# Attention in plain float32 for two heads at once on halves of the PE array

## The chip, the core and the metric

The kernel runs on one core of a Trainium2 chip, as a single launch. The metric is the device time of one execution in microseconds (us). The engines are called as in the profile: PE is the matmul engine and PEld its weight loads, DVE the vector engine, ACT the scalar engine, POOL the third elementwise engine, SP the one that issues the DMAs. The program holds its tiles in on-chip memory of 128 partitions, and PE writes its results to eight accumulator banks (PSUM) of 512 float32 per partition.

## The reference

Eight batches of eight heads, head dimension 64, with 512 local tokens and 32 global tokens. A local query sees the 32 global keys and the local keys at most 32 positions away. A global query sees all 544 keys. The heads of a token then form a row of 512 numbers, and all 8 x 544 = 4,352 rows go through a gated feed-forward network (the FFN).

```
k_all = concatenate([k_g, k_l]); v_all = concatenate([v_g, v_l])
out_g = softmax(scale * q_g @ k_all.T) @ v_all
s_ll  = where(|i - j| <= 32, scale * q_l @ k_l.T, -1e9)
out_l = softmax(concatenate([scale * q_l @ k_g.T, s_ll])) @ v_all
x     = concatenate([out_g, out_l]), heads side by side: rows of 512
gate  = 1 / (1 + exp(-(x @ w_gate)))          # w_gate, w_val: 512 x 1536
out   = (gate * (x @ w_val)) @ w_out          # w_out: 1536 x 512
```

Inputs and output are float32. The weights reach the device as 64-bit words that it turns into float32 itself.

## The kernel before

**Precision on PE.** A matmul of plain float32 operands appears in the trace as two passes over the same moving columns, each with its own weight load. An operand in the rounded type fp32r takes one. The kernel therefore writes a number as hi + lo, two fp32r parts, and makes a product of three fp32r matmuls (hi hi, lo hi, hi lo). The FFN is made that way throughout: `xt` holds the transposed activations and `wg`, `wv`, `wo` the weights, each with a hi and a lo half.

**Chunks.** The local tokens are cut into nine chunks: chunk 0 and chunk 1 are the first and second 256 tokens of batch 0, and chunks 2 to 8 are batches 1 to 7 of 512 tokens. The 256 global rows of all batches form a last FFN chunk. The FFN of a chunk runs over 12 slices `f` of the 1,536 hidden columns. For each slice there are 12 matmuls into `bank_g`, 12 into `bank_v` (L721) and, one slice later, 3 per block of 128 tokens into `bank_o` (L735). For 512 tokens this makes 36 matmuls of 512 columns for a slice, 432 for a chunk. Between them stand the gate (ACT: tanh, exp, abs), the value (DVE: two operations), `hh` hi (ACT) and `hh` lo (POOL).

**Attention** of a chunk is done while PE runs the FFN of the chunk before it. A `local_unit` is one head and two blocks of 128 queries: scores of each block against a window of 192 or 224 keys (L345), masked maximum (`reduce`, L392), exp (L405), sums and their inverse (L356, L357), normalising, transposing the probabilities, and the product with v (`pv`). A `global_unit` is one head: 32 global queries against all keys (`sa`, L546, and `gg`, L339), softmax on 32 partitions, transposing, and the product with v (`gp`, L493).

There are two forms. Chunks 0 and 1 and the first four heads of chunk 2 are *native*: float32 operands, q and k on 64 partitions (the even head of a pair on the lower half, the odd one on the upper half), and probabilities turned by PE (L424, L425, then a copy from PSUM). The other 52 heads are *split*: ACT and POOL cut q and k (L287 to L293) and v (L319, L321) into hi and lo, so that 128 partitions hold q hi and q lo. The probabilities are transposed in 32 x 32 blocks by DVE (`tb`), written to DRAM (`pd`) and read back in the turned order (`pt`), then cut into hi and lo as well (L467, L469). `pv` uses v hi and v lo side by side as 128 weight columns and moves p hi and p lo, 256 columns. Its two halves of partitions and columns are added by ACT, DVE and POOL (L480 to L484). For 52 heads `gp` of one head is interleaved with `sa` of the next. At the end of a pair of heads `x_split` cuts the transposed attention output into the hi and lo of `xt` (L600, L602).

**Weights.** 36 blocks of weight words (12 slices of `w_gate`, `w_val`, `w_out`) are loaded and turned into hi and lo in `convert`: two operations of DVE (L235, L236), one of ACT (L238), one of DVE (L240), one of ACT (L249), one of POOL (L251). Three word buffers and two output buffers are shared by all blocks. The FFN of chunk 0 uses a slice as soon as it is there; chunk 1 and the rest find all of them.

**What sets the order.** The class `Order` simulates five engines with a written cost per step, takes the step that can start first, and emits it. Steps may ask for named resources (`att`: four PSUM banks, `s`: three score buffers, `pt`, `tb` and so on). The FFN advances a count called progress, one for each four matmuls of 512 columns, 108 for a chunk of 512 tokens and 54 for each of chunks 0 and 1. Attention steps are released at given progress: before the change chunk 2 from 19 on, one unit each 3; a later chunk from 7 before the start of the chunk ahead of it, one unit each 4. Each engine executes its emitted instructions in that order.

## Time and profile before

| | us |
|---|---|
| median of 3 runs | 1157.84 (1156.86 to 1164.7) |
| the profiled execution | 1152.93 |
| its span, first to last instruction | 1151.2 |
| PE busy | 1114.6 (97%) |
| ACT, DVE, POOL busy | 774.6, 727.0, 708.0 |

The mean granted clock of the execution is 0.992. A row of the timeline gives the start, the time from the first start to the last end, engine, line, operation, output and inputs, the size (weights as rows * columns, then the moving partitions x columns) and how many instructions are merged in it. Ends of matmuls overlap the next start, so the pitch of PE is read from start to start. A row of the windows gives a stretch, its length, the busy time of PE, PEld, DVE, ACT and POOL with the number of instructions, the granted clock, the share of the DMA engines and GB/s. A row of the groups gives line, engine, operation, names, shapes and count, then busy time, the mean duration of one in ns, and the idle time before them.

### The profile page before, as it was taken

How to read it: one execution, taken by the hardware profiler on the slowest of the kernel's cores; microseconds unless marked ns; L12 is line 12 of the kernel's file. 1: busy time of each engine (PE TensorE's matmuls, PEld its weight loads, DVE VectorE, ACT ScalarE, POOL GpSimd, SP SyncE). 2: the span in 40 equal slices, each digit the busy share in tenths (PEclk: the TensorE clock that was granted, in tenths of full speed). 3: DMA queues.
4: the chain of work that ended last, by engine and by line, in shares of the span. 5: the costliest groups of instructions: out<-in, count | busy, mean ns of one | idle time of the engine just before them, and what ended most of it. 6: DMA issues, size and time to landing. Idle time of an engine off the chain costs nothing.

```text
span 1151.2 us, 20677 instructions
## 1 busy us (share of the span) xinstructions
PE 1114.6 (97%) x6190; PEld 924.7 (80%) x6190; DVE 727.0 (63%) x2627; ACT 774.6 (67%) x1835; POOL 708.0 (62%) x735
## 2 busy tenths in 40 slices
PE   7899999999999999999999999999999999999998
PEld 5687778878887887887788787888788878888897
DVE  5778967767774777577766777577757777211122
ACT  6778977767875777677766777677776776422232
POOL 2445456777876777777867778778776787311111
PEclk9799999999999999999999999999999999999999
DMA  6667838767665765576656765586567664221143
GB/s 234 225 214 230 259 113 241 213 178 201 181 171 144 218 179 156 163 224 180 167 167 184 195 176 155 165 225 182 165 174 209 171 190 142 83 70 67 56 165 110
DMA packets 177200, 199.83 MB, mean 174 GB/s; under 512 B 108992, under 2 KB 136640, under 8 KB 177088
## 3 DMA queue, kind: packets, MB, share of 16 engines
q1 hardware_dynamic: 177088, 198.51, 58.7%
q8 instruction: 49, 0.80, 0.3%
q14 instruction: 63, 0.52, 0.1%
HBM read 159.38 MB, written 39.06 MB: 172 GB/s over the span
## 4 chain that ended last, share of the span: by engine, by line
PE 74%; issue 6%; POOL 6%; ACT 5%; DMA 5%; DVE 3%; SPq 1%; POOLq 0%; DVEq 0%; ACTq 0%
PE bank_g L721 20%; PE bank_v L721 20%; PE bank_o L735 19%; PE bank_x L345 4%; PE bank_x L546 3%; DMA qk_raw<-in_qk_dram 2%; PE bank_x L476 2%; PE bank_x L477 2%; POOL hh L676 2%; PE bank_x L493 1%; POOL pt L469 1%; POOL kl L290 1%; PE bank_x L441 1%; DMA xt<-in_w_val_dram 1%; POOL qk_hi L293 1%
## 5 line engine op out<-in xcount | busy, mean ns | idle before, releaser
L721 PE MATMUL bank_v<-xt,wv 128*128 128x512 f32 (+1 forms) x1440 | 321.9, 364 | 7.1 <-ACT ex L660 5.9
L721 PE MATMUL bank_g<-xt,wg 128*128 128x512 f32 (+1 forms) x1440 | 321.8, 366 | 4.2 <-ACT xt L600 3.5
L735 PE MATMUL bank_o<-wo,hh 128*128 128x512 f32 x1224 | 316.0, 395 | 0.8 <-POOL hh L676 0.5
L721 PEld LDWEIGHTS bank_g<-xt,wg 128*128 128x128 f32 x1440 | 242.3, 190 | 51.4 <-ACT xt L600 4.4
L721 PEld LDWEIGHTS bank_v<-xt,wv 128*128 128x128 f32 x1440 | 237.7, 189 | 52.1 <-ACT ex L660 8.9
L735 PEld LDWEIGHTS bank_o<-wo,hh 128*128 128x128 f32 x1224 | 221.0, 188 | 45.3 <-POOL hh L676 1.9
L676 POOL TENSOR_TENSOR hh<-th,hh 128x512 fp32r<-128x512 f32 (+1 forms) x120 | 135.2, 1126 | 197.7 <-ACT hh L674 193.1
L670 DVE SCALAR_TENSOR_TENSOR bank_v<-ex,bank_v 128x512 f32<-128x512 f32 (+1 forms) x120 | 72.7, 606 | 150.6 <-PE bank_v L721 143.2
L469 POOL TENSOR_TENSOR pt<-pt 128x512 fp32r<-128x512 f32 x104 | 134.5, 1294 | 28.5 <-ACT pt L467 22.0
L674 ACT CAST hh<-th 128x512 fp32r<-128x512 f32 (+1 forms) x120 | 66.4, 553 | 110.5 <-DVE th L671 101.8
L405 ACT ACTIVATE s_buf<-s_buf,nm 128x192 f32<-128x192 f32 (+1 forms) x248 | 113.9, 462 | 18.7 <-DVE nm L392 18.3
L659 ACT ACTIVATE th<-bank_g 128x512 f32<-128x512 f32 (+1 forms) x120 | 64.0, 533 | 86.1 <-PE bank_g L721 84.1
L392 DVE CUSTOM_DVE_ANT_0 s_buf<-bank_x,masks 128x192 f32<-128x192 f32 (+1 forms) x248 | 82.0, 367 | 55.9 <-PE bank_x L345 55.6
L290 POOL TENSOR_TENSOR kl<-qk_raw,qk_hi 128x736 fp32r<-128x736 f32 x52 | 92.5, 1779 | 33.9 <-ACT qk_hi L287 27.3
L484 POOL TENSOR_TENSOR x<-t 64x256 f32<-64x256 f32 x104 | 76.1, 732 | 45.4 <-DVE t L482 33.2
L482 DVE TENSOR_TENSOR t<-bank_x,t 64x512 f32<-64x512 f32 x104 | 70.3, 676 | 43.7 <-ACT t L480 43.1
L361 DVE TENSOR_SCALAR_CACHE_REDUCE s_buf<-s_buf,r 128x224 f32<-128x224 f32 (+1 forms) x223 | 87.2, 427 | 3.7
L321 POOL TENSOR_TENSOR vhl<-v_raw,vhl 128x512 fp32r<-128x512 f32 x52 | 67.1, 1290 | 32.9 <-ACT vhl L319 15.7
L480 ACT COPY t<-bank_x 64x512 f32<-64x512 f32 x104 | 60.6, 583 | 34.5 <-PE bank_x L477 19.2
L293 POOL TENSOR_TENSOR qk_hi<-qk_raw,qk_hi 64x256 fp32r<-64x256 f32 x104 | 78.4, 774 | 4.1
L671 DVE SCALAR_TENSOR_TENSOR th<-th,bank_v 128x512 f32<-128x512 f32 (+1 forms) x120 | 72.9, 607 | 11.3 <-ACT th L662 0.4
L287 ACT CAST qk_hi<-qk_raw 128x1280 fp32r<-128x1280 f32 x52 | 65.6, 1261 | 16.6 <-DMA qk_raw<-in_qk_dram 15.4
(122 smaller groups left out, 1874.6 us busy)
## 6 DMA issues: line engine op xcount, KB each, us to landing
wo<-wo_dram SPq DMA_DIRECT2D x108, 512.0 KB, 3.4
qk_raw<-in_qk_dram SPq DMA_DIRECT2D x104, 320.0 KB, 4.7
pt<-pd SPq DMA_DIRECT2D x208, 128.0 KB, 3.1
pd<-tb SPq DMA_DIRECT2D x416, 56.0 KB, 2.2
v_raw<-in_v_dram SPq DMA_DIRECT2D x52, 256.0 KB, 3.4
...
```

The lines of the kernel that those rows point to most:

```text
L290: nc.gpsimd.tensor_tensor(kl, t[:, K0:Q1], hi[:, K0:Q1].bitcast(F32), op=ALU.subtract)
L293: nc.gpsimd.tensor_tensor(hi[64:128, r], t[64:128, r], hi[64:128, r].bitcast(F32), op=ALU.subtract)
L361: nc.vector.tensor_scalar(p, p, r, None, op0=ALU.mult, op1=ALU.add, accum_out=total)
L392: nc.vector.tensor_tensor_reduce(out=s_sb[:, i, 0:w], in0=s_ps[:, i, 0:w], in1=masks[:, m:m + w], scale=-0.125, scalar=3.0e38, op0=ALU.add ...
L405: nc.scalar.activation(s_sb[:, i, 0:w], s_sb[:, i, 0:w], AF.Exp, bias=nm[:, i:i + 1], scale=-1.0, accum_out=sm[:, i:i + 1])
L469: nc.gpsimd.tensor_tensor(flat[:, 1], flat[:, 1].bitcast(F32), flat[:, 0].bitcast(F32), op=ALU.subtract)
L484: nc.gpsimd.tensor_tensor(x_part(T, x32s, col0), t0[:, :, 0], t0[:, :, 1], op=ALU.add)
L670: nc.vector.scalar_tensor_tensor(acc, ex, 1.0, acc, op0=ALU.min, op1=ALU.mult)
L671: nc.vector.scalar_tensor_tensor(th, th, 1.0, acc, op0=ALU.add, op1=ALU.mult)
L676: nc.gpsimd.tensor_tensor(hh[:, 1, 0:ntok], th, hh[:, 0, 0:ntok].bitcast(F32), op=ALU.subtract)
L721: nc.tensor.matmul(acc, w[a][:, t, fs], xt[:, c, t, x0:x0 + ntok], start=n == 0, stop=n == 11)
L735: nc.tensor.matmul(C2["o"][t], ph[:, a, t * P:(t + 1) * P], pwo[:, c], start=f2 == 0 and i == 0, stop=f2 == NF - 1 and i == 2)
```

## The change

All attention becomes native, and two heads go through PE together. The functions `keys`, `local_scores`, `x_part`, `invert`, `normalise`, `products`, `finish`, `last_products` and `x_split` disappear. `convert`, `gate`, `value`, `put_out` and `ffn_stream` stay as they were, apart from naming their PSUM bank by its slot.

- `local_unit` takes a pair of heads. The even head's q and k lie on partitions 0 to 63, the odd head's on 64 to 127; the score matmuls (now L312) alternate between the halves and write to two banks. In `pv` (now L398) all 128 partitions of probabilities are moved, the even head's product goes to PSUM partitions 0 to 63 and the odd head's to 64 to 127 of one bank, so each uses 64 of the array's columns.
- Chunks 0 and 1 turn the probabilities by PE, as before; all the others (chunk 2 too) by DVE and DRAM, but in float32 and without cutting them.
- `xt` hi and lo are made straight from PSUM (L402 on ACT or DVE, L404 on DVE). POOL keeps the `hh` lo and the weights.
- `global_unit` takes four heads, whose 32 queries each lie on four groups of 32 partitions of the same bank; softmax, five full 128 x 128 transposes and one `gp` serve all four.
- Chunk 2's attention is released from progress 40, one unit each 6; later chunks one unit each 10. Three buffers of 4 x 224 scores, one `tb`, three of qk and of v.

The core of the diff:

```diff
-EARLY = {0: (-1000, 1), 1: (-900, 1), 2: (19, 3)}
-BASE, PER = -7, 4
-HOLE = (8, 1)
+EARLY = {0: (-1000, 1), 1: (-900, 1), 2: (40, 6)}
+BASE, PER = -7, 10
...
+        yield (st := step("scores", "PE", cold + 1.0, take=["att", "att", "s"], give=qk_over(T), after=[when(("qk", ci, pr))]))
+        slots, si = st["slots"]["att"], st["slots"]["s"][0]
+        s_ps = [bank([P, 2, 256], "bank_s", i) for i in slots]
...
         for i, j in enumerate(blocks):
-            qj = ks[0][:, qcol(j) - q0:qcol(j) - q0 + P]
-            for t, (kt, k0) in enumerate(zip(ks, k0s)):
-                js = slice(k0 + KOFF[j], k0 + KOFF[j] + KWIN[j])
-                nc.tensor.matmul(s_ps[:, i, 0:KWIN[j]], qj, kt[:, js], start=t == 0, stop=t == last)
+            for e in range(2):
+                js, qj = K0 - q0 + KOFF[j], qcol(j) - q0
+                nc.tensor.matmul(s_ps[e][:, i, 0:KWIN[j]], half(t, e)[:, qj:qj + P], half(t, e)[:, js:js + KWIN[j]],
+                                 start=True, stop=True)
...
+        yield (st := step("pv", "PE", 1.1, take=["att"] + (["xt"] if new and ci != 1 else []), give=["pt"] + v_over(T),
...
+        for i, j in enumerate(blocks):
+            side = KWIN[j] - (WIN - P)
+            for w, rows in ((VM[j], P), (VS[j], side)):
+                for e in range(2):
+                    out, p = half(o_ps, e)[:, i], moving(e, i, 0 if rows == P and w == VM[j] else 1)[0:rows]
...
+                    nc.tensor.matmul(out, vt[0:rows, e, w, :], p, start=w == VM[j], stop=w == VS[j])
+        xt, xs = xts[key], slice(T["x0"] + col0, T["x0"] + col0 + 2 * P)
+        flat = o_ps.rearrange("p i c -> p (i c)")
+        yield (st := step("x hi", {"ACT": 0.33, "DVE": 0.36}))
+        (nc.scalar.copy if st["on"] == "ACT" else nc.vector.tensor_copy)(xt[:, 0, pr, xs], flat)
+        yield step("x lo", "DVE", 0.4, give=freed(slot))
+        nc.vector.tensor_tensor(xt[:, 1, pr, xs], flat, xt[:, 0, pr, xs].bitcast(F32), op=ALU.subtract)
...
+        heads = [(half(T["qk"], e), 64 * i + 32 * e) for i, T in enumerate(pair) for e in range(2)]
+        for part in range(2):
...
+            for t, p in heads:
...
+                nc.tensor.matmul(sa[p:p + 32, 2 * part:2 * part + 2], t[:, QK - SG - q0:QK - q0], view, start=True, stop=True)
...
+        for i, T in enumerate(pair):
+            vt = group["v", T["pr"]]
+            for j in range(5):
+                for e in range(2):
+                    nc.tensor.matmul(half(og, e)[:, i], vt[:, e, (VM + VS)[j], :], ptg[:, j, 64 * i + 32 * e:64 * i + 32 * e + 32],
+                                     start=j == 0, stop=j == 4)
```

How the order of instructions moves is seen at three places. In these rows stand the line, the operation, output and inputs, and the size; `x4` merges four equal ones.

PE before, in the FFN of chunk 0, where the units of two native heads happen to follow each other (L425 turns probabilities, L345 is scores, L441 is `pv`):

```order
L425 MATMUL bank_y<-ident,s_buf_107 128x128
L345 MATMUL bank_x<-qk_nat 128x192
L345 MATMUL bank_x<-qk_nat 128x224
L345 MATMUL bank_x<-qk_nat 128x192
L345 MATMUL bank_x<-qk_nat 128x224
L441 MATMUL bank_x<-pt_nat,v_nat 64x128
```

The first two rows of L345 are one head, the next two the other head, on the other half of the partitions. Elsewhere before, one head stands alone; after, each group holds two heads, one row for both heads' matmuls of a block:

```order
L312 MATMUL bank_s<-qk 128x224 x2
L312 MATMUL bank_s<-qk 128x192 x2
L398 MATMUL bank_x<-pt,v 64x128 x16
L312 MATMUL bank_s<-qk 128x224 x2
L312 MATMUL bank_s<-qk 128x192 x2
```

PE in the FFN of a later chunk, before: one head's scores and one head's `pv` between the products of `bank_v`.

```order
L721 MATMUL bank_v<-xt,wv_119 128x512 x4
L345 MATMUL bank_x<-qk_hi 128x192
L345 MATMUL bank_x<-kl,qk_hi 128x192
L345 MATMUL bank_x<-qk_hi 128x224
L345 MATMUL bank_x<-kl,qk_hi 128x224
L476 MATMUL bank_x<-pt,vhl 128x256
L477 MATMUL bank_x<-pt,vhl 128x256
L476 MATMUL bank_x<-pt,vhl 128x256
L477 MATMUL bank_x<-pt,vhl 128x256
L721 MATMUL bank_v<-xt,wv_118 128x512 x4
```

The same engine after, in the FFN of chunk 2 (L572 and L586 are the FFN's lines now, L427 `sa`, L429 `gg`, L452 and L453 transposes, L467 `gp`, all for four heads):

```order
L572 MATMUL bank_v<-xt,wv_116 128x512 x4
L427 MATMUL bank_sa<-qk 32x256 x8
L429 MATMUL bank_gg<-qk 32x32 x4
L572 MATMUL bank_v<-xt,wv_115 128x512 x4
L586 MATMUL bank_o<-wo,hh 128x512 x12
L572 MATMUL bank_g<-xt,wg_113 128x512 x4
L452 MATMUL bank_y<-ident,pg_buf 128x128 x4
L453 MATMUL bank_z<-ident,pg_buf 128x128
L572 MATMUL bank_g<-xt,wg_114 128x512 x4
L572 MATMUL bank_g<-xt,wg_113 128x512 x4
L467 MATMUL bank_og<-ptg,v 64x32 x20
L398 MATMUL bank_x<-pt,v 64x128 x8
```

Groups of scores, `sa`, `gg`, `gp` and `pv` stand between full-array matmuls of the FFN, fewer and larger than before.

DVE before, in the second half of the weight conversion (L235, L236, L240 are the conversion, L670 and L671 the FFN's value, the rest attention of chunks 1 and 2):

```order
L235 TENSOR_SCALAR bank_w<-xt 128x512
L236 SCALAR_TENSOR_TENSOR bank_w<-xt,bank_w 128x512
L561 TENSOR_SCALAR mg<-sg 32x1
L562 RECIPROCAL mg<-mg 32x1
L240 SCALAR_TENSOR_TENSOR xt<-xt,bank_w 128x512
L235 TENSOR_SCALAR bank_w<-xt 128x512
L236 SCALAR_TENSOR_TENSOR bank_w<-xt,bank_w 128x512
L444 COPY x_1184<-bank_x 64x256
L240 SCALAR_TENSOR_TENSOR xt<-xt,bank_w 128x512
L392 ISA s_buf_107,nm<-bank_x,masks 128x224
```

After, in the same part (L231, L232 and L236 are the conversion, L520 and L521 the value):

```order
L236 SCALAR_TENSOR_TENSOR xt<-xt,bank_w 128x512 x2
L520 SCALAR_TENSOR_TENSOR bank_v<-ex,bank_v 128x256
L521 SCALAR_TENSOR_TENSOR th<-th,bank_v 128x256
L231 TENSOR_SCALAR bank_w<-xt 128x512
L232 SCALAR_TENSOR_TENSOR bank_w<-xt,bank_w 128x512
L236 SCALAR_TENSOR_TENSOR xt<-xt,bank_w 128x512
L231 TENSOR_SCALAR bank_w<-xt 128x512
L232 SCALAR_TENSOR_TENSOR bank_w<-xt,bank_w 128x512
L231 TENSOR_SCALAR bank_w<-xt 128x512
L232 SCALAR_TENSOR_TENSOR bank_w<-xt,bank_w 128x512
L236 SCALAR_TENSOR_TENSOR xt<-xt,bank_w 128x512 x2
```

The attention of chunks 0 and 1 is over by then and that of chunk 2 has not begun, so only conversion and value remain.

560 lines of the change are left out of this document (196 added, 364 removed).

## The prediction

> **What bounds the kernel now.** I read the engine totals first, then the windows between the output stores, then single stretches of PE's timeline. The rows show the engine totals, five windows, and the issues of the output stores.
>
> ```profile
> PE 1114.6 (97%) x6190; PEld 924.7 (80%) x6190; DVE 727.0 (63%) x2627; ACT 774.6 (67%) x1835; POOL 708.0 (62%) x735
> ...
> 0.00:47.00 47.00, 34.97 (x188) 27.13 (x189) 31.74 (x107) 32.96 (x89) 15.35 (x31) 0.89 0.70 241
> 47.00:155.00 108.00, 106.58 (x738) 84.78 (x736) 88.24 (x276) 91.17 (x248) 48.85 (x46) 0.98 0.69 222
> 174.50:250.30 75.80, 71.28 (x505) 63.58 (x504) 52.32 (x206) 55.60 (x142) 53.80 (x58) 1.00 0.76 215
> 377.60:502.50 124.90, 122.70 (x646) 101.99 (x645) 87.35 (x331) 90.67 (x207) 93.61 (x97) 1.00 0.64 180
> ...
> 1010.00:1090.00 80.00, 80.00 (x347) 1.00 0.19 66
> ...
> 174.40 0.88 SPq L693 DMA_DIRECT2D out_dram<-ob  x2
> 250.24 0.81 SPq L693 DMA_DIRECT2D out_dram<-ob  x2
> 377.57 1.30 SPq L693 DMA_DIRECT2D out_dram<-ob  x3
> 879.64 1.42 SPq L693 DMA_DIRECT2D out_dram<-ob  x3
> 1098.79 1.44 SPq L693 DMA_DIRECT2D out_dram<-ob  x3
> ```
>
> PE is busy nearly throughout, so what changes the length of its queue changes the time. The stretch from 1010 to 1090 holds the FFN alone: 80/347 = 0.2305 us per 512-column matmul, so a chunk's 432 take 99.6 us. Chunks 3 to 6 end every (879.64 - 377.57)/4 = 125.5 us; the other 26 us are attention and waits. The last stretch, from 1001 on, holds no attention and does not change.
>
> The FFN of chunk 0 stands out: it begins at 47 and stores at 174.40, although its matmuls (12 slices of 24 half-length and 6 whole ones) need only 12 x (24 x 0.115 + 6 x 0.2305) = 50 us. It waits for weights, the last of which is finished at 155:
>
> ```profile
> L251 POOL TENSOR_TENSOR wo<-xt,wo x12: 1269/1278/1301, 28.0 to 155.0; 128x512 fp32r<-128x512 f32 x12
> ```
>
> PE was not idle in that time, because the slow native attention of chunks 0, 1 and half of 2 filled it.
>
> **What attention costs PE now, and what two at once cost.** These rows of PE's timeline are the split form (scores, `pv`, global, each with the row behind it), then the native form.
>
> ```profile
> 208.20 0.25 PE L345 MATMUL bank_x<-qk_hi 128*128 128x192 f32 x1
> ...
> 208.64 1.56 PE L735 MATMUL bank_o<-wo,hh 128*128 128x512 f32 x6
> ...
> 213.89 0.31 PE L476 MATMUL bank_x<-pt,vhl 128*128 128x256 f32 x1
> ...
> 214.40 1.09 PE L735 MATMUL bank_o<-wo,hh 128*128 128x512 f32 x4
> ...
> 217.61 0.19 PE L493 MATMUL bank_x<-ptg,vhl 128*128 128x64 f32 x1
> ...
> 218.24 0.71 PE L721 MATMUL bank_v<-xt,wv 128*128 128x256 f32 x4
> ...
> 107.99 0.97 PE L345 MATMUL bank_x<-qk_nat 64*128 64x224 f32 x4
> 108.94 0.88 PE L493 MATMUL bank_x<-ptg_nat,v_nat 128*64 128x32 f32 x10
> 109.75 0.74 PE L721 MATMUL bank_v<-xt,wv 128*128 128x256 f32 x4
> 110.42 1.05 PE L546 MATMUL bank_x<-qk_nat 64*32 64x256 f32 x4
> 111.40 1.19 PE L721 MATMUL bank_v<-xt,wv 128*128 128x256 f32 x8
> ...
> 114.50 0.27 PE L424 MATMUL bank_y<-ident,s_buf 128*128 128x128 f32 x1
> 114.61 0.27 PE L425 MATMUL bank_y<-ident,s_buf 128*128 128x128 f32 x1
> 114.82 0.98 PE L345 MATMUL bank_x<-qk_nat 64*128 64x192 f32 x8
> 115.73 0.43 PE L441 MATMUL bank_x<-pt_nat,v_nat 128*64 128x128 f32 x2
> 116.00 0.38 PE L442 MATMUL bank_x<-pt_nat,v_nat 128*64 128x128 f32 x2
> 116.21 0.38 PE L441 MATMUL bank_x<-pt_nat,v_nat 128*64 128x128 f32 x2
> ```
>
> Split, per head: scores of two blocks 0.44, `pv` 0.51, global 0.63 plus two short `gg` (0.05). A chunk has 16 units and 8 globals: 16 x 0.95 + 8 x 0.68 = 20.6 us. With the FFN that is 120.2, so 5.3 of the 125.5 us are waits; 2.2 of them show as idle PE (124.90 - 122.70).
>
> Native, two things show. First, four score passes of one head take 0.95 us (107.99 to 108.94), and eight passes of two heads on the two halves take 0.91 (114.82 to 115.73): both halves of the rows work at once. Second, a change between full and part array costs about 0.1: L425 begins 0.11 after L424, but the part-array L345 begins 0.21 after L425. The Trainium skill ("TensorE: Matmul & The Clock Gate", section "Part 3: Packing small matmuls") has matmuls start and end strictly in program order. The trace disagrees: the program has one head's four passes ahead of the other's, and the eight still fit the time of four. By that rule the odd head's half would start one pass late in each group, an estimate of 8 x (0.2 + 0.1) = 2.4 us more per chunk than the sum below.
>
> After, per chunk on PE:
> - scores, 8 groups of two heads: from the expected end of L425 (114.72) to 115.73, 1.01 with both changes of array: 8.1, against 16 x 0.44 = 7.0 before.
> - `pv`, 8 groups. One head's pass is (116.21 - 116.00)/2 = 0.105, and there are 8 for it. If the column halves run together as the row halves do, 8 x 0.105 plus 0.06 at the start (115.73 to 116.00 is 0.27, not 0.21) plus two changes is 1.10: 8.8, against 8.2 before. If they take turns, 1.94. No row of before has both column halves in use, so the bounds are these two. I take the first, by the nearest row, that of the row halves.
> - `sa`: a pass is (111.40 - 110.42 - 0.1)/4 = 0.22. Four heads have 16, on four separate quarter-width parts. All four at once: 4 x 0.22, with `gg` and changes 1.2. By row halves alone 2.15. One at a time 4.1. I take 1.2, since parts that share neither rows nor output partitions are the same case as the row halves, and keep the rest as rivals.
> - `g turn`, five full transposes: 0.54. `gp`: a short pass is (0.81 - 0.2)/10 = 0.06; 20 pairs and the changes 1.4, or 2.6 in turn.
> - Two globals of four heads: 2 x 3.1 = 6.3, against 5.4.
>
> Sum 23.2, which is 2.6 more than before: plain float32 is no cheaper for PE in a later chunk. It has to come from waits. Of 5.3 us, those on the added halves, on `pt` lo and on `xt` (POOL, and ACT's splits) have no instruction any more. POOL keeps only `hh` lo; ACT and DVE lose the splits, the additions and most of the small softmax. I take 2 us of waits left, between 0.5 and 5.3. A later chunk is then 99.6 + 23.2 + 2 = 124.8, a change of -0.7 (-2.2 to +2.6), and chunks 3 to 7 give -3.5 (-11 to +13). The write and read of `pd` and the loads on SP are further ahead than before (one unit each 10 of progress instead of each 4, two heads in it), so I cost them at nothing: the FFN's matmuls of some 10 us between two units hide them. If that cover is gone, `pv` stands at the head of PE's queue until `pt` has landed, the FFN behind it, and the 2 us grow.
>
> **The first 250 us.** The end of the conversion sets the end of chunk 0. It needs DVE most:
>
> ```profile
> L236 DVE SCALAR_TENSOR_TENSOR bank_w<-xt,bank_w 128x512 uint32<-128x512 uint32 x36 | 25.1, 696 | 1.2
> L235 DVE TENSOR_SCALAR bank_w<-xt 128x512 uint32<-128x512 uint32 x36 | 24.7, 685 | 6.9 <-DMA xt<-in_w_val_dram 3.0 <-DMA xt<-in_w_gate_dram 2.8 <-ACT x L444 0.9
> L240 DVE SCALAR_TENSOR_TENSOR xt<-xt,bank_w 128x512 uint32<-128x512 uint32 x36 | 24.0, 677 | 5.0 <-POOL wo L251 2.3 <-POOL wg L251 1.2 <-ACT xt L238 0.8
> L392 DVE CUSTOM_DVE_ANT_0 s_buf<-bank_x,masks 128x224 f32<-128x224 f32 x124 | 47.3, 382 | 14.7 <-PE bank_x L345 14.5
> L392 DVE DVE_READ_ACCUMULATOR2_ANT nm<- 128x1 f32 x256 | 21.0, 82 | 0.0
> L356 DVE TENSOR_SCALAR r<-sm 128x1 f32<-128x1 f32 x256 | 31.6, 146 | 36.6 <-ACT s_buf L405 35.0
> L670 DVE SCALAR_TENSOR_TENSOR bank_v<-ex,bank_v 128x256 f32<-128x256 f32 x36 | 15.2, 422 | 45.0 <-PE bank_v L721 40.2 <-ACT ex L660 3.8 <-ACT pg_buf L564 1.0
> ```
>
> A block costs 0.685 + 0.696 + 0.677 = 2.06 of DVE, 36 of them 74. Before, DVE is busy 31.74 + 88.24 = 120 us until 155, which is 77% of the time. After, it must do until then: 74; for 8 units of two heads four reduces (0.382 + 0.082), five small operations of 0.146 and one x lo (as L670, 0.42), 3.0 each, 24; value of chunk 0, 12 x 2 x 0.42 = 10; two globals, 3. Together 111, and some of the normalising and copying that either engine may do, say 3. The half of chunk 2's attention that lay in this time (and 6 of 8 global softmaxes) is gone from it. At 77% this ends at 114/0.77 = 148, with a full DVE at 114. In the second half only conversion and value are left in DVE's queue, 3 x 2.06 + 0.84 = 7.0 us a slice, where a slice now takes (155.0 - 28.0)/11 = 11.5. I take 141, nearer to the first, since ACT and the two output buffers stay in the chain of each block. PE has no backlog of attention then: chunk 0 stores some 4 us later instead of 19.4, at 145.
>
> Against this stands the clock. PE will idle between slices, and a short idle costs clock: here 2.81 us of work in 5 were followed by a window at 0.55 and one at 0.50 (columns: window, length, PE, PEld, DVE, ACT, POOL, clock):
>
> ```profile
> 35.00:40.00 5.00, 2.81 (x20) 2.05 (x18) 3.99 (x7) 3.15 (x6) 2.02 (x2) 1.00 0.90 311
> 40.00:45.00 5.00, 4.97 (x20) 3.22 (x20) 4.57 (x17) 3.12 (x8) 3.23 (x3) 0.55 0.79 271
> 45.00:50.00 5.00, 4.04 (x19) 3.53 (x18) 3.27 (x9) 3.71 (x9) 0.73 (x1) 0.50 0.65 213
> ```
>
> At half clock a slice of chunk 0 takes 8.4 us instead of 4.2, about what conversion takes too, so PE still keeps up, and only the last slice is late. DVE's value steps wait for PE, and the next block's words are queued behind them. I take 1.5 us: chunk 0 stores at 146.5, -28 (-20 to -34).
>
> Chunk 1 then needs 50 us of FFN and all of chunk 2's attention but the quarter that is released before (from 40 of 54, over 60): 17 to 18, and 3 of waits: 71 against 75.8, -5. Chunk 2 took 377.57 - 250.24 = 127.3; like the others now, 124.8, -2.5.
>
> **Sum.** -28 - 5 - 2.5 - 3.5 = -39 against the profiled 1152.93: 1114. The median of the runs is 4.9 us above that execution, so 1157.84 - 39 = 1119 for the runs.
>
> **The rivals.**
> 1. *Column halves take turns.* Nothing in the trace shows them together, and both halves read the same 128 partitions, unlike the row halves. `pv` grows by 8 x 0.84, `gp` by 2 x 1.2: 9.1 us a chunk. In chunks 0 and 1 PE has room for it; for the seven chunks 2 to 8 it is 64: 1183, slower. It decides once the halves overlap less than four tenths (39 of 64 lost). Chance 0.10.
> 2. *`sa` runs two at a time.* Fourteen globals x 0.95 = +13: 1132. Chance 0.12.
> 3. *`sa` runs one at a time*, because all four heads write to one bank; the score matmuls, which overlap in the trace, write to two. 14 x 2.9 = +41: 1160, no change. Chance 0.06. The Trainium skill ("TensorEngine Tiling (Array Packing)", section "Restrictions and Gotchas") says that different row tiles cannot access the same PSUM bank simultaneously, which speaks for this; no run here shows it yet.
> 4. *The conversion does not speed up:* DVE stands at value steps for a PE at half clock. Early gain 10 instead of 28: 1137. Chance 0.10.
>
> **How the numbers follow.** The forecast has 0.62 with its own range of 1104 to 1136 (the early gain by +8 or -6, the later chunks by -8 or +12 to either side). With rivals 2 and 4 it gives faster 0.84; rival 3 is 0.06 for within 1%; rival 1 is 0.10 for slower. The runs of before spread over 0.7%, so about 1% can be told from no change. The range is 1104 to 1142: it leaves out rivals 1 and 3 and a little of the edges.
>
> **What will show it.** Right: the last weight block ends near 141 and chunk 0 stores near 146; eight `pv` passes' time for sixteen (L398 about 1.1 us from start to start with its changes); `sa` with `gg` about 1.2; later chunks end each 124 to 126 us; POOL busy falls below 250. Wrong: L398 near 1.9, L427 at 2 or more, a last weight block after 150, or PE idle in the later chunks on `pt` read back late.

## The result and the profile after

The changed kernel takes 1121.22 us (median of 4 runs, 1118.58 to 1123.63); the kernel before, run beside it, 1157.35 (4 runs, 1156.65 to 1164.70). The ratio is 0.967 with a 95% interval of 0.963 to 0.972. The profiled execution after took 1118.58 with a span of 1116.6; before, 1152.93 and 1151.2. The spans are 34.6 us apart.

The engine totals on the page after:

```profile
PE 1079.9 (97%) x6838; PEld 859.7 (77%) x6838; DVE 530.1 (47%) x1864; ACT 492.1 (44%) x1297; POOL 182.8 (16%) x171
```

A window of before that the prediction did not show, from 47 to the store of chunk 0:

```profile
47.00:174.40 127.40, 125.98 (x879) 100.21 (x878) 100.26 (x329) 104.33 (x288) 57.42 (x54) 0.99 0.62 202
```

The windows after: the start, from 47 to the store of chunk 0, the second half of the conversion, chunk 1, and chunk 3:

```profile
0.00:47.00 47.00, 34.76 (x328) 27.64 (x329) 37.11 (x163) 37.15 (x110) 10.85 (x22) 0.93 0.77 260
47.00:144.30 97.30, 77.31 (x529) 65.82 (x528) 80.51 (x190) 66.75 (x157) 45.88 (x41) 0.88 0.74 246
60.00:136.00 76.00, 56.01 (x308) 47.17 (x307) 62.88 (x128) 50.49 (x111) 39.36 (x35) 0.84 0.79 266
144.30:219.40 75.10, 75.10 (x664) 64.01 (x664) 43.51 (x181) 39.14 (x126) 8.81 (x12) 1.00 0.79 251
345.10:469.90 124.80, 124.80 (x764) 96.61 (x763) 57.89 (x220) 51.39 (x137) 15.48 (x12) 1.00 0.52 161
```

After, the issues of the output stores, from the timeline, and then the group of the `wo` weight blocks on POOL, with the durations and the first and last start:

```profile
144.30 1.04 SPq L543 DMA_DIRECT2D out_dram<-ob  x2
219.43 0.87 SPq L543 DMA_DIRECT2D out_dram<-ob  x2
345.14 1.46 SPq L543 DMA_DIRECT2D out_dram<-ob  x3
469.91 1.45 SPq L543 DMA_DIRECT2D out_dram<-ob  x3
844.54 1.45 SPq L543 DMA_DIRECT2D out_dram<-ob  x3
```

```profile
L247 POOL TENSOR_TENSOR wo<-xt,wo x12: 1276/1286/1299, 23.7 to 136.2; 128x512 fp32r<-128x512 f32 x12
```

PE's busy time fell by 1114.6 - 1079.9 = 34.7 us, as much as the span. That the two agree is chance: up to the store of chunk 1 PE's busy time fell by 45 us (232.2 to 187.2) and the time by 30.8, and behind it PE's busy time rose by 10 while the time fell by 3.8. Most of the gain lies ahead of the store of chunk 0: 174.40 became 144.30, which is 30.1 of the 34.6. Chunk 1 takes 75.1 after it (before 75.8), chunk 2 125.7 (127.3), chunks 3 to 6 (844.54 - 345.14)/4 = 124.85 each (125.5). The last weight block begins at 136.2 instead of 155.0, which is 18.8 of the 30.1; the other 11.3 are the way from there to the store, 8.1 instead of 19.4. Of the 18.8, 5.1 are there when the fourth `wo` block begins (66.6 instead of 71.7); the other 13.7 come from there to the last block, which takes 69.6 us instead of 83.3.

The limit of this stage changed. Before, from 47 to the store, PE stood idle for 1.4 us of 127.4. After, it stands idle for 20 of 97.3, with the clock at 0.84 from 60 to 136, and waits for weights. These are the rows of the waits from 60 to 125, PE's and then those of the DMA queue (a load of weight words, L222, waits for the last DVE operation on its buffer):

```profile
PE bank_g L572 <- POOL wg L247: 9.5, 7, 2.0
...
PE bank_g L572 <- ACT wg L245: 6.3, 5, 2.1
```

```profile
SPq L222 <- DVE xt L236: 39.4, 18, 5.5
```

In the later chunks (345 to 845) the view of waits has no row for PE's matmuls at all. The groups of two and four heads are these, in the timeline of PE after:

```profile
347.79 1.56 PE L572 MATMUL bank_v<-xt,wv 128*128 128x512 f32 x6
349.27 1.10 PE L398 MATMUL bank_x<-pt,v 128*64 128x128 f32 x16
350.30 1.20 PE L586 MATMUL bank_o<-wo,hh 128*128 128x512 f32 x4
351.43 0.97 PE L312 MATMUL bank_s<-qk 64*128 64x192 f32 x8
352.33 0.96 PE L586 MATMUL bank_o<-wo,hh 128*128 128x512 f32 x3
...
372.62 2.14 PE L586 MATMUL bank_o<-wo,hh 128*128 128x512 f32 x8
374.69 1.07 PE L427 MATMUL bank_sa<-qk 64*32 64x256 f32 x16
375.58 0.24 PE L429 MATMUL bank_gg<-qk 64*32 64x32 f32 x8
375.75 3.06 PE L572 MATMUL bank_g<-xt,wg 128*128 128x512 f32 x12
...
383.95 1.10 PE L398 MATMUL bank_x<-pt,v 128*64 128x128 f32 x16
384.88 1.31 PE L467 MATMUL bank_og<-ptg,v 128*64 128x32 f32 x40
386.12 0.73 PE L586 MATMUL bank_o<-wo,hh 128*128 128x512 f32 x2
```

Sixteen `pv` passes of two heads take 350.30 - 349.27 = 1.03 us; sixteen `sa` passes of four heads 375.58 - 374.69 = 0.89, with `gg` 1.06; forty `gp` passes 1.24.

### The profile page after: what moved, and what is told of

It reads as the page before. It is cut to its first block, busy times and chain, and to the rows that moved or that the text cites. A ratio compares the mean times of both kernels' runs of the same rounds, so it can differ in the third digit from the quotient of the medians.

```text
span 1116.6 us, 18791 instructions
## 1 busy us (share of the span) xinstructions
PE 1079.9 (97%) x6838; PEld 859.7 (77%) x6838; DVE 530.1 (47%) x1864; ACT 492.1 (44%) x1297; POOL 182.8 (16%) x171
## 4 chain that ended last, share of the span: by engine, by line
PE 84%; issue 4%; DMA 2%; POOL 1%; DVE 1%; ACT 0%; POOLq 0%; DVEq 0%; ACTq 0%
PE bank_v L572 24%; PE bank_g L572 24%; PE bank_o L586 23%; PE bank_x L398 5%; PE bank_s L312 5%; DMA xt<-in_w_gate_dram 2%; PE bank_og L467 2%; PE bank_sa L427 1%; POOL hh L526 1%; PE bank_y L452 1%; DMA xt<-in_w_out_dram 1%; DVE xt L236 0%; POOL wo L247 0%; POOL wg L247 0%; DVE bank_w L231 0%
## 5 line engine op out<-in xcount | busy, mean ns | idle before, releaser
L572 PE MATMUL bank_g<-xt,wg 128*128 128x512 f32 (+1 forms) x1296 | 301.7, 377 | 19.5 <-POOL wg L247 11.6
L586 PE MATMUL bank_o<-wo,hh 128*128 128x512 f32 x1224 | 314.0, 398 | 0.3 <-ACT hh L524 0.2
L572 PE MATMUL bank_v<-xt,wv 128*128 128x512 f32 (+1 forms) x1296 | 301.0, 379 | 1.3 <-POOL wv L247 0.7
L572 PEld LDWEIGHTS bank_g<-xt,wg 128*128 128x128 f32 x1296 | 226.8, 191 | 73.9 <-POOL wg L247 13.3
L572 PEld LDWEIGHTS bank_v<-xt,wv 128*128 128x128 f32 x1296 | 226.7, 193 | 53.0 <-issue 8.6
L586 PEld LDWEIGHTS bank_o<-wo,hh 128*128 128x128 f32 x1224 | 224.5, 189 | 55.0 <-issue 8.3
L520 DVE SCALAR_TENSOR_TENSOR bank_v<-ex,bank_v 128x512 f32<-128x512 f32 (+1 forms) x120 | 73.8, 615 | 257.6 <-PE bank_v L572 244.1
L524 ACT CAST hh<-th 128x512 fp32r<-128x512 f32 (+1 forms) x120 | 66.8, 557 | 163.4 <-DVE th L521 163.1
L321 DVE CUSTOM_DVE_ANT_0 s_buf<-bank_s,masks 128x192 f32<-128x192 f32 (+1 forms) x256 | 81.0, 370 | 104.6 <-PE bank_s L312 104.5
L340 DVE TENSOR_SCALAR_CACHE_REDUCE s_buf<-s_buf,r 128x192 f32<-128x192 f32 (+1 forms) x215 | 80.9, 426 | 1.7
L521 DVE SCALAR_TENSOR_TENSOR th<-th,bank_v 128x512 f32<-128x512 f32 (+1 forms) x120 | 73.0, 608 | 15.6 <-ACT pg_buf L442 0.5
L398 PE MATMUL bank_x<-pt,v 128*64 128x128 f32 (+1 forms) x1024 | 71.2, 279 | 0.2 <-ACT pt L358 0.2
L398 PEld LDWEIGHTS bank_x<-pt,v 128*64 128x64 f32 (+1 forms) x1024 | 55.0, 136 | 19.4 <-issue 11.6
L512 ACT ACTIVATE th<-th 128x512 f32<-128x512 f32 (+1 forms) x120 | 68.2, 568 | 0.0
L312 PE MATMUL bank_s<-qk 64*128 64x192 f32 (+1 forms) x512 | 64.4, 366 | 0.4 <-DVE xt L404 0.4
L365 DVE STREAM_TRANSPOSE tb<-s_buf 128x896 f32<-128x896 f32 x56 | 62.2, 1110 | 3.2 <-DMA pd<-tb 0.7
L510 ACT ACTIVATE ex<-bank_g 128x512 f32<-128x512 f32 (+1 forms) x120 | 63.6, 530 | 0.0
L312 PEld LDWEIGHTS bank_s<-qk 64*128 64x128 f32 x512 | 42.9, 188 | 21.2 <-issue 13.9
L404 DVE TENSOR_TENSOR xt<-bank_x,xt 128x256 fp32r<-128x256 f32 x64 | 26.9, 422 | 67.0 <-ACT xt L402 66.9
```

The costliest lines, as they stand in the source:

```text
L312: nc.tensor.matmul(s_ps[e][:, i, 0:KWIN[j]], half(t, e)[:, qj:qj + P], half(t, e)[:, js:js + KWIN[j]], start=True, stop=True)
L321: nc.vector.tensor_tensor_reduce(out=s_sb[:, 2 * e + i, 0:w], in0=s_ps[e][:, i, 0:w], in1=masks[:, m:m + w], scale=-0.125, scalar=3.0e38, ...
L340: nc.vector.tensor_scalar(src, src, r[:, k:k + 1], None, op0=ALU.mult, op1=ALU.add, accum_out=sm[:, k:k + 1])
L398: nc.tensor.matmul(out, vt[0:rows, e, w, :], p, start=w == VM[j], stop=w == VS[j])
L512: nc.scalar.activation(th, th, AF.Abs)
L520: nc.vector.scalar_tensor_tensor(acc, ex, 1.0, acc, op0=ALU.min, op1=ALU.mult)
```

## The experiments

All in one table first: when the last `wo` block begins on POOL, the stores of chunks 0, 1 and 2 in the profiled execution, and the time. Where there is a ratio it is to the kernel before run beside it, whose median was 1157 to 1163 us in the several sets. The stores are those of one execution, and the changed kernel's four runs spread over 5 us, so differences of a few us between two rows are read from the stages and not from the time.

| kernel | last block | chunk 0 | chunk 1 | chunk 2 | time, us | ratio (95%) |
|---|---|---|---|---|---|---|
| before | 155.0 | 174.40 | 250.24 | 377.57 | 1157.35 | |
| after | 136.2 | 144.30 | 219.43 | 345.14 | 1121.22 | 0.967 (0.963 to 0.972) |
| b_late | 156.8 | 172.24 | 278.69 | 403.70 | 1172.32 | 1.012 (1.006 to 1.019) |
| b_split_late | 163.4 | 172.10 | 278.27 | 404.36 | 1188.78 | 1.027 (1.021 to 1.034) |
| a_early | 143.2 | 156.77 | 224.38 | 348.93 | 1121.94 | 0.967 (0.963 to 0.971) |
| a_double1 | 144.7 | 152.44 | 227.64 | 353.35 | 1127.44 | one run |
| a_noword | 132.1 | 138.64 | 214.36 | 340.07 | 1113.17 | one run |
| a_words4 | 131.5 | 143.56 | 219.18 | 344.88 | 1116.11 | 0.958 (0.955 to 0.961) |
| a_words4_warm | 130.0 | 142.35 | 217.68 | 343.39 | 1116.64 | 0.964 (0.957 to 0.971) |
| a_lead9 | 177.8 | 202.91 | 223.16 | 347.67 | 1121.96 | 0.967 (0.959 to 0.975) |
| a_lead6 | 175.3 | 190.09 | 220.65 | 345.15 | 1118.46 | 0.964 (0.957 to 0.970) |
| a_words4_l8 | 167.6 | 188.22 | 213.00 | 337.50 | 1112.06 | 0.961 (0.955 to 0.966) |
| a_samecols | 145.2 | 158.35 | 239.62 | 372.24 | 1180.20 | one run |
| a_headorder | 140.0 | 146.78 | 226.51 | 356.69 | 1152.58 | one run |

### Does the kernel before gain by the later release alone, or by splitting all of chunk 2?

```diff
-EARLY = {0: (-1000, 1), 1: (-900, 1), 2: (19, 3)}
+EARLY = {0: (-1000, 1), 1: (-900, 1), 2: (40, 2.5)}
```

> The kernel before with one number pair changed: chunk 2's attention released from progress 40, one step each 2.5, instead of 19 and 3, so that it lies behind most of the weight conversion, as in the changed kernel. Theory (the early gain is PE's shorter queue, since one-head native attention is gone): nothing of PE's work goes away here, and PE had only about 6 us of idle time between 47 and 250, so chunk 0 stores some 10 to 20 us earlier, chunk 1 takes as much longer, chunk 1's store stays within 4 us of 250, and the total stays within 5 us of 1157. Rival (the gain comes from the later release alone, by taking chunk 2's work out of DVE's queue during the conversion): chunk 1 stores at 225 to 235 and the total falls to 1130 to 1140.

And with the same release, `NATIVE_HEADS = 0` instead of 4:

> The kernel before with the later release (progress 40, one step each 2.5) and with the first four heads of chunk 2 in the split form like all other heads of the later chunks. Theory: PE loses 8 native local units (about 2.2 us against 0.95) and 4 native globals (about 2.4 against 0.7), together about 17 us of a queue that was full, so chunk 2 stores 8 to 17 us earlier and the total is 1140 to 1149: half or less of the gain of the changed kernel, the rest being the one-head native work of chunks 0 and 1. Rival (splits of q, k, v on ACT and POOL were what held the early stage): with four more heads to split nothing is gained or it gets slower, 1155 to 1170.

Both take longer than before, b_late by 1.2% and b_split_late by 2.7%. Both expectations of the theory missed: the first had put the total within 5 us of 1157 and chunk 1's store within 4 us of 250, the second (1140 to 1149) is off by 40 us. The rival of the first, a gain from the later release alone, missed as well. In the profiled execution moving alone gives chunk 0 only 2 us. But in b_late's profile the first `wo` block began at 38.1 instead of 28.0; the instructions of all engines are in the order of before up to there, and its other three runs were 8 to 13 us shorter than the profiled one, so that is not the edit's. Without those 10 us chunk 0 would store some 12 us earlier than before, an estimate that agrees with the theory's 10 to 20. From the fourth to the last weight block it needed 74.9 us against 83.3 before. So chunk 2's attention did slow the conversion, by about 8 us. But chunk 1 then takes 106.5 us instead of 75.8. The first row shows that stage of b_late: of the 30.7 us, 20.0 are PE's busy time (91.28 instead of 71.28, with chunk 2's attention in it and the clock at 0.89), and 10.6 are idle time. Where PE is idle stands in its waits, of b_late from 230 to 280, then of b_split_late from 60 to 280; the last row is a window over b_split_late's chunk 1, where POOL is busy for 76.58 us:

```profile
172.30:278.70 106.40, 91.28 (x605) 78.91 (x606) 62.31 (x253) 71.53 (x185) 63.06 (x68) 0.89 0.58 163
```

```profile
PE bank_x L476 <- POOL pt L469: 9.4, 2, 7.9
```

```profile
PE bank_x L476 <- POOL pt L469: 19.4, 9, 6.8
```

```profile
174.50:278.30 103.80, 79.62 (x527) 70.80 (x526) 69.00 (x279) 72.81 (x181) 76.58 (x84) 0.85 0.69 187
```

`pv` waits for the lo half of the probabilities from POOL. A later chunk of before keeps POOL busy for 93.6 us; a chunk 1 of 75 us can't hold that. This speaks for the following reading, which is argued from the waits and not shown by a run of its own: the split form can't be squeezed into the early stage; the native form, which needs no POOL, can, but fills PE. The two-head form asks nothing of POOL for attention and less of PE than native. For the second run the rival holds, by more than it had said: splitting more heads makes it slower. That PE's queue had been full is not contradicted, since these two kernels traded it for another wait.

### Is the place of chunk 2's attention what matters?

```diff
-EARLY = {0: (-1000, 1), 1: (-900, 1), 2: (40, 6)}
+EARLY = {0: (-1000, 1), 1: (-900, 1), 2: (19, 7)}
```

> The changed kernel with chunk 2's attention released from progress 19, one unit each 7, instead of 40 and 6, about where the kernel before released it. Theory (the conversion, paced by DVE, now ends chunk 0, and PE idles about 20 us beside it): some four units of two heads enter DVE's queue in the conversion, about 5 us of DVE each, so chunk 0 stores 8 to 20 us later, chunk 1 takes 6 to 9 us less (PE work of those units now lies in its idle time), and the total is 1121 to 1133. Rival (the conversion's loads set its pace and DVE has room): chunk 0's store moves by less than 4 us and the total falls by 4 to 8, to 1113 to 1117.

Chunk 0 stores 12.5 us later, chunk 1 takes 67.6 instead of 75.1, and the time is the same (1121.94 and 1121.22). This is as the theory had it. The release moves work between the two stages; it is not where the gain comes from.

### Does PE's queue still count in the first stage?

In the four loops that issue scores, `pv`, `sa` and `gp`, each matmul of chunk 1's attention stands twice:

```diff
-            for e in range(2):
+            for e in [0, 1] * (2 if ci == 1 else 1):
```

> The changed kernel with every matmul of chunk 1's attention (scores, pv, sa, gp) issued twice, with the same results: 4 x (0.9 + 1.0) + 2 x (0.9 + 1.2) = 11.8 us more of PE inside the weight conversion, nothing more on DVE, ACT or in the loads. Theory (PE idles about 20 us beside the conversion, so PE's queue no longer sets the end of chunk 0): chunk 0 stores 0 to 4 us later than 144.3 and the total is 1121 to 1126. Rival (PE's queue still sets it, and the gain is simply PE time saved in the first 250 us): chunk 0 or chunk 1 ends 10 to 12 us later and the total is 1130 to 1134.

Chunk 0 stores 8.1 us later, between the two expectations and nearer to the rival. The rows of POOL's fourth `wo` block show where, first after, then with the doubled matmuls:

```profile
66.62 1.29 POOL L247 TENSOR_TENSOR wo<-xt,wo 128x512 fp32r<-128x512 f32 x1 [3.02 <-ACT wo L245]
```

```profile
75.43 1.30 POOL L247 TENSOR_TENSOR wo<-xt,wo 128x512 fp32r<-128x512 f32 x1 [3.87 <-ACT wo L245]
```

All 8.8 us are there by the fourth block. From it to the last block it takes 69.2 us, against 69.6 in the changed kernel. The last of the doubled groups starts at 70.1. So until about 70 us, while attention of chunks 0 and 1 goes through PE, DVE and ACT, PE's time counts. Of the time after that this run says nothing, since no doubled matmul lies there; that PE waits for weights there shows in its 20 us of idle time.

### What sets the pace of the conversion after that?

One of DVE's two first operations on a block left out:

```diff
-        nc.vector.tensor_scalar(v, high, 0x80000000, None, op0=ALU.bitwise_and)
-        nc.vector.scalar_tensor_tensor(v, low, 29, v, op0=ALU.logical_shift_right, op1=ALU.bitwise_or)
+        nc.vector.tensor_scalar(v, low, 29, None, op0=ALU.logical_shift_right)
```

> The changed kernel with one of DVE's three operations for a weight block left out: the sign bit is not taken over, so all weights are positive and the output is not the reference's; the loads, the other operations and the FFN are the same. It takes 36 x 0.69 = 25 us from DVE, 17 of them after 60. Theory (DVE sets the pace of the conversion, 63 of 76 us busy from 60 to 136): the last weight block ends 10 to 17 us earlier, at 120 to 127 instead of 137, chunk 0 stores at 127 to 135, the total is 1101 to 1111. Rival (the three word buffers and their loads set the pace): the last block ends less than 5 us earlier and the total stays within 5 us of 1121.

This kernel leaves out the sign of the weights. Of DVE's work after 60, 17 us are gone, and the last block comes only 4.1 us earlier, as the rival had it; 2.1 of the 4.1 are there at the fourth block already (64.5 instead of 66.6). The profiled execution is 1118.58 - 1113.17 = 5.4 shorter; the time of 1113.17 lies between the two expectations. DVE is the busiest engine there (62.88 of 76), but its busy time does not set the pace. The next candidate was the loop of a word buffer, since the loads wait 39.4 us of 65 for a buffer:

```diff
-    conv_bufs = [words[:, i * 1024:(i + 1) * 1024] for i in range(3)]
-    conv_out = [words[:, 3072 + i * 512:3072 + (i + 1) * 512] for i in range(2)]
+NW, NO = 4, 2
...
+    conv_bufs = [words[:, i * 1024:(i + 1) * 1024] for i in range(NW)]
+    conv_out = [ffn.tile([P, 512], U32, name="xt", tag="ob", bufs=3) for i in range(NO)]
```

> The changed kernel with four word buffers for the weight conversion instead of three (the two output buffers move into the not yet used output tiles). Theory, new after the run without one DVE operation (the loop of one word buffer sets the pace: load about 5 us from issue to landing, three DVE steps and one of ACT with their queues, three buffers): loads are issued a block earlier, DVE no longer waits for them, slices from the fourth to the last take 7.3 to 8 us each instead of 8.7, the last weight block ends at 128 to 133 instead of 137.5, the total falls to 1111 to 1117. Rival (the DMA engines are the limit, 0.7 to 0.8 busy in this stretch): the last block ends at 136 or later and the total stays within 4 us of 1121.

The last block begins 4.7 us earlier; from the fourth on a slice takes (131.5 - 67.7)/8 = 7.98 us instead of (136.2 - 66.6)/8 = 8.70. That is the theory's reading, at its weak end. The time is 1116.11 and the ratio 0.958, just below the interval of the changed kernel, which was measured in another set. Yet the profiled executions show only 0.7 us of it at chunk 0's store, since the way from the last block to there grew from 8.1 to 12.1. So the number of buffers is a part of the pace. The rest is not settled; with a DMA share of 0.96 from 80 to 100 in this kernel a fifth buffer may not help, which was not tried.

Whether the clock makes that last stretch long was the next question. Ten matmuls on old weights, whose result is overwritten, stand ahead of each of the slices 3 to 11:

```diff
+                            if C["ci"] == 0 and f >= 3 and which == 0:
+                                for i in range(10):
+                                    nc.tensor.matmul(acc, wg[0][:, i % KT, 0:P], xt[:, 0, i % KT, x0:x0 + ntok], start=True, stop=True)
```

> The kernel with four word buffers, and in chunk 0's FFN ten more matmuls of 256 columns ahead of each of the slices 3 to 11: they use old weights, write to the accumulator that the slice's first matmul then overwrites, and wait for nothing of the conversion; the result is the same. About 9 x 1.15 = 10 us of PE in time that was idle. In the kernel with four word buffers the clock from 120 to 140 was 0.75 and chunk 0 stored 10.8 us after the last weight block, against 6.8 with three. Theory (the clock falls because PE idles between slices, and the last slices then run slowly): the clock between 80 and 140 is 0.95 or more, chunk 0 stores 5 to 7 us after the last weight block, at 137 to 140, total 1110 to 1114. Rival (the added matmuls lie ahead of the slices in PE's queue and delay them, or the clock falls all the same): chunk 0 stores no earlier than 143, total 1116 to 1124.

The clock from 120 to 140 was 0.83 instead of 0.75, the way from the last block to the store 12.4 instead of 12.1, and the time the same (1116.64 and 1116.11). The time is the rival's, and chunk 0's store at 142.35 lies between the two expectations (137 to 140, and 143 or later). But the run does not test what it was made for. These are PE's wait in the last slice and the stretch behind it, first of a_words4, then with the added matmuls:

```profile
130.26 3.44 PE L575 MATMUL bank_v<-xt,wv 128*128 128x256 f32 x12 [2.93 <-ACT wv L248]
```

```profile
130.00:136.00 6.00, 5.61 (x20) 4.47 (x22) 3.17 (x8) 1.57 (x4) 3.24 (x3) 0.51 0.69 213
```

```profile
128.76 0.79 PE L578 MATMUL bank_v<-xt,wv 128*128 128x256 f32 x4 [2.89 <-ACT wv L248]
```

```profile
130.00:136.00 6.00, 5.89 (x21) 4.51 (x22) 2.16 (x6) 0.41 (x1) 2.02 (x3) 0.50 0.82 251
```

The added matmuls stand ahead of `bank_g`, while the last long wait, 2.9 us, lies between `bank_g` and `bank_v`. So it stayed, and with it the six us at half clock behind it. PE works through nearly all of them, and but for 0.1 us in a_words4 and 0.6 in a_words4_warm it has no further wait until the store. At full clock the same work would take about half, so the clock costs close to 3 us there, an estimate. In a_words4 these six us lie behind the start of the last block (131.5), in the changed kernel ahead of it (136.2), where the clock is 1.00 from 137 to 143; that is the larger part of the 4 us by which the way to the store grew with the fourth buffer. Whether a filled wait would keep the clock up is not shown.

### Can PE's idle time be used?

`LEAD = 9` and `LEAD = 6` instead of 12: the FFN of chunk 1 begins inside the conversion.

> The changed kernel with the FFN of chunk 1 begun inside the weight conversion: chunk 0 runs slices 0 to 8, chunk 1 the same slices, then both in turn for slices 9 to 11, and those last three slices are converted without an accumulator bank as scratch. Theory (conversion ends chunk 0, and PE idles some 20 us beside it): PE fills part of that idle time with chunk 1's slices, chunk 1 stores at 207 to 215 instead of 219.4, total 1109 to 1117. Rival (the conversion is slowed by chunk 1's value steps on DVE and by the missing scratch banks): chunk 1 stores at 217 to 230, total 1119 to 1132.

> The same with six slices ahead instead of nine: half of chunk 1's FFN (25 us of PE) may run inside the conversion, which fills all of PE's idle time there. Theory: chunk 1 stores at 200 to 212, total 1102 to 1114, faster than with nine. Rival: six slices without scratch banks and with chunk 1's value steps between them delay the last weight block from 137 to 150 or later; chunk 1 stores no earlier than with nine.

Neither gains more than its interval: 1121.96 and 1118.46. With nine the rival held; with six chunk 1 stores 2.5 us earlier than with nine, still outside the theory. The conversion of the last slices is slow (last block at 175 to 178); whether by the missing scratch banks or by chunk 1's steps between them is not taken apart. And a new wait appears in front of chunk 2. This is PE's row in a_lead6 from 170 to 222:

```profile
PE bank_x L398 <- DMA pt<-pd: 12.3, 3, 4.9
```

It is the wait that the prediction had costed at nothing as long as the FFN covers it. Here less FFN is left to cover it. The last run joined four word buffers and three output buffers with `LEAD = 8` and a release of chunk 2 from 30:

> Four word buffers and three output buffers, eight slices of chunk 0 and then of chunk 1 before the last four in turn, and chunk 2's attention released from progress 30 instead of 40 (with six and nine slices ahead PE waited some 12 and 8 us for chunk 2's probabilities to be read back, just before chunk 2). Theory: those waits go, PE's idle time in the conversion is filled, chunk 1 stores at 205 to 213 instead of 219, total 1102 to 1110. Rival (the slices without scratch banks, 13 to 15 us each instead of 9, and the earlier chunk 2 delay the conversion): chunk 1 stores at 217 or later, total 1115 to 1125.

```profile
PE bank_x L401 <- DMA pt<-pd: 9.2, 2, 6.5
```

1112.06 us (1110.56 to 1113.82). It is the lowest time of all, between the two expectations; the wait for `pt` is still there, 9.2 us from 170 to 215. It lies below the changed kernel in every run, by 9 us of the medians, though the two were not run side by side and the intervals of their ratios overlap by a little. In the profiled executions 6.4 us of it are there at chunk 1's store.

### What are the halves of the columns worth?

Both heads' `pv` to PSUM partitions 0 to 63:

```diff
-        o_ps = bank([P, 2, P], "bank_x", slot)
+        o_ps = bank([64, 2, 2, P], "bank_x", slot)
...
-                    out, p = half(o_ps, e)[:, i], moving(e, i, 0 if rows == P and w == VM[j] else 1)[0:rows]
+                    out, p = o_ps[:, e, i], moving(e, i, 0 if rows == P and w == VM[j] else 1)[0:rows]
```

> The changed kernel with the probability products of both heads of a pair on the same half of the array's columns: both results go to PSUM partitions 0 to 63, side by side, and are then taken from there to xt by twice as many copies of half the partitions. Theory (in the changed kernel the two column halves run at the same time): the group of 16 passes takes about 1.95 us instead of 1.10, which is 8 x 0.84 = 6.7 us for a chunk and 47 for chunks 2 to 8; a later chunk takes 131 to 132 instead of 124.9, the total 1165 to 1172. Rival (the halves took turns already, or PE has room): no change beyond 5 us.

```profile
376.37 1.97 PE L398 MATMUL bank_x<-pt,v 128*64 128x128 f32 x16
378.26 1.21 PE L589 MATMUL bank_o<-wo,hh 128*128 128x512 f32 x4
...
372.24 1.43 SPq L546 DMA_DIRECT2D out_dram<-ob  x3
...
899.23 1.45 SPq L546 DMA_DIRECT2D out_dram<-ob  x3
```

A group takes 378.26 - 376.37 = 1.89 us instead of 1.03, and a chunk (899.23 - 372.24)/4 = 131.75, 6.9 more. Over the stages of chunks 1 to 7 this is (1027.73 - 158.35) - (966.32 - 144.30) = 47.4 us, as expected. Another 14.1 lie ahead of chunk 0's store, which nobody had priced. They can't be put down to PE alone: the edit also doubles the copies to `xt`, of half the partitions each, and the groups of attention stand in another order there. In this single run the time is 1180.2, above the kernel before.

### Does the order of the heads' matmuls matter?

In the four groups all matmuls of one head come ahead of the next head's:

```diff
-        for i, j in enumerate(blocks):
-            for e in range(2):
+        for e in range(2):
+            for i, j in enumerate(blocks):
```

> The changed kernel with PE's instructions of a group in another order: all matmuls of one head, then all of the next head, in scores, pv, sa and gp, instead of the heads in turn. Theory (a matmul may pass an earlier one that uses other rows, columns or quarters of the array, as the eight score passes of two heads in the trace of before, which stood one head behind the other and took the time of four): each group takes the same time to 0.2 us, a later chunk 124 to 127, total 1116 to 1135. Rival (matmuls begin strictly in program order, so only the last pass of a head overlaps the first of the next): scores 0.7, pv 0.7, sa and gp together 2 to 4 us longer each, 16 to 19 us a chunk, total 1230 or more.

```profile
421.69 1.59 PE L398 MATMUL bank_x<-pt,v 128*64 128x128 f32 x16
423.21 0.96 PE L572 MATMUL bank_g<-xt,wg 128*128 128x512 f32 x3
...
448.49 1.09 PE L427 MATMUL bank_sa<-qk 64*32 64x256 f32 x16
449.38 0.26 PE L429 MATMUL bank_gg<-qk 64*32 64x32 f32 x8
...
356.69 1.78 SPq L543 DMA_DIRECT2D out_dram<-ob  x3
...
874.18 1.42 SPq L543 DMA_DIRECT2D out_dram<-ob  x3
```

Neither expectation: a chunk takes (874.18 - 356.69)/4 = 129.4, 4.5 more. `sa` is unchanged at 0.89 and so are the scores (0.91 against 0.90, medians of chunks 3 to 6); `pv` takes 423.21 - 421.69 = 1.52 instead of 1.03, which is 8 x 0.49 = 3.9 of the 4.5. In all, this order costs 1152.58 - 1118.58 = 34 us between the two profiled executions, about as much as the whole change gained, by a single run. Where a head has four passes, the next head's start at once; where it has eight, they don't. The starts of the 16 `pv` passes, in ns from the first (from single records of the trace, the groups at 383.95 in the changed kernel and at 421.69 in this one; in the second row a pass is put to a head by its distance of about 110 to the head's pass before):

```
heads in turn:      0   7 | 160 167 | 270 276 | 379 385 | 488 495 | 597 604 | 706 713 | 820 826
one head, the next: 0 160 270 383 491 | 497 603 657 711 766 820 880 | 988 1100 1208 1316
```

The second head's first pass starts at 497, together with the first head's fifth (491), when three of the first head's passes have not started. With four passes a head, three have not started either when the next head begins. So passes of another part of the array may overtake; that they do so past three waiting ones of a part and no more fits both cases.

## Why the prediction was right, and where it was not

**The sum.** Forecast -39 against the profiled execution, measured 1152.93 - 1118.58 = -34.4; 1119 for the runs, measured 1121. That the last two are only 2 us apart is in part luck: the sum is 4.6 off (chunk 1 gave 4 us less than forecast, chunk 0 2 more), and the median of the changed kernel lies 2.6 above its profiled execution, where 4.9 had been added.

**Chunk 0, -28 (-20 to -34).** Measured -30.1. The last block was put at 141 and began at 136.2; the way to the store was put at 5.5 and took 8.1. That PE's backlog goes was right: idle 1.4 us before, 20 after. The step that failed is the reason for the conversion's pace, "it needs DVE most": with 25 us of DVE's work gone the last block came only 4.1 us earlier, with one more word buffer 4.7. So the 77% of DVE's time that the estimate rested on did not mark the limit. A part of the limit is the loop of the word buffers (8.70 us a slice with three, 7.98 with four); the rest stays open. That the number came out nearly right is luck in part: chunk 2's attention in the conversion did cost time, 8 us by b_late and 7 by a_early, but why, if DVE's busy time does not set the pace, is not shown. Less in DVE's queue may also let that loop turn faster; this is argued.

The clock was put at 1.5 us. These rows of the changed kernel show the stretch ahead of the store, and what PE does behind it:

```profile
130.00:136.00 6.00, 5.15 (x22) 5.05 (x23) 4.65 (x17) 5.30 (x17) 2.08 (x2) 0.50 0.69 253
```

```profile
138.17 1.08 PE L572 MATMUL bank_g<-xt,wg 128*128 128x256 f32 x8
139.19 1.10 PE L398 MATMUL bank_x<-pt,v 128*64 128x128 f32 x16
...
142.15 1.55 PE L586 MATMUL bank_o<-wo,hh 128*128 128x512 f32 x6
```

PE has no wait from 130.85 to the store, and 5.15 us of that are at half clock. Half of it, 2.6 us, is the most that a full clock could have saved; but the last `wv` block ends on POOL only at 133.4, and behind that 2.7 us are left at half clock, so about 1.4 us is the nearer estimate, close to the 1.5. The slow stretch ends as the last block begins, so the 8.1 us are another term that was too small: the plain 4 us of way, which had been put without parts. In PE's order the first 24 products of chunk 1 and a `pv` group stand ahead of the last six of chunk 0, and these alone take 142.15 - 138.17 = 4.0 us.

**Chunk 1, -5; measured -0.7.** The step that failed is the sum of 50 us of FFN, 17 to 18 of attention and 3 of waits. These are PE's groups of the FFN in that stretch (144.3 to 219.4), with shapes kept apart:

```profile
L586 PE MATMUL bank_o<-wo,hh 128*128 128x512 f32 x72 | 19.9, 402 | 0.0
L572 PE MATMUL bank_v<-xt,wv 128*128 128x256 f32 x132 | 18.2, 282 | 0.0
L572 PE MATMUL bank_g<-xt,wg 128*128 128x256 f32 x127 | 17.8, 284 | 0.0
...
L572 PE MATMUL bank_g<-xt,wg 128*128 128x512 f32 x15 | 3.8, 396 | 0.0
...
L572 PE MATMUL bank_v<-xt,wv 128*128 128x512 f32 x12 | 3.2, 404 | 0.0
```

By pitch this is 259 x 0.115 + 72 x 0.2305 + 27 x 0.2305 = 52.6 us, since 27 matmuls of chunk 2's FFN lie ahead of chunk 1's store and only some 29 of chunk 1's shorter ones ahead of chunk 0's. The estimate summed the work of one chunk and set it against an interval between stores, which is not the same where chunks of unlike length follow each other: 2.6 us. The remaining 75.1 - 52.6 = 22.5 us are attention and its changes of array, where 20.5 had been put with the waits. PE has no wait there; of attention the stretch holds seven groups of scores (two of them chunk 3's already), seven of `pv` and both global units, where three quarters of a chunk's had been put.

**Chunk 2, -2.5; measured -1.6. Chunks 3 to 7, -0.7 each; measured -0.65 for chunks 3 to 6** and 0.0 for chunk 7 (966.32 - 844.54 = 121.8 both times). The 2 us of waits that were kept are no waits, since PE has none there. They lie in the changes of the array: the eight L586 from 372.62 would let the next start at 372.62 + 8 x 0.2305 = 374.46, and `sa` starts at 374.69; 0.23 where 0.1 had been counted. So a chunk is 99.6 + 25.2, as forecast, with the 25.2 all of it PE's: the total came out because two errors cancel, waits that are not there and changes that were priced too low.

**The rivals.** Column halves in turn: no, 1.03 us a group. Forced for `pv` alone, it cost the 47 us that had been priced for `pv` (7 x 8 x 0.84), and 14 more in the first stage, where PE had been said to have room (with other edits of that run in it). `sa` two at a time or one at a time: no, 0.89 us for 16 passes. For the second of these the Trainium skill ("TensorEngine Tiling (Array Packing)", section "Restrictions and Gotchas") had been cited, by which different row tiles cannot access the same bank simultaneously. Here the four heads, on two row halves, write to four groups of 32 partitions of one bank, and their passes run together; the trace disagrees. The reason given for the 1.2 of `sa` was not sound, though: with two row halves for four heads, two of them always share their rows, so `sa` needed parts of the columns to run together just as `pv` did. The conversion does not speed up: it did, by 18.8 us. By the rule of strict program order in the Trainium skill ("TensorE: Matmul & The Clock Gate", section "Part 3: Packing small matmuls") 2.4 us more a chunk had been estimated; with the heads in turn none of it shows, and with one head behind the other the starts follow the rule for `pv` in part and for scores and `sa` not at all.

**The range and the chances.** 1104 to 1142 held 1121.2; the time is faster by over 1%, which was put as by far the likeliest.
